# Linear attention and a Mish layer, gated: both halves of a block's query products in one group, E transposed in place, wo later

## The chip, the cores and the metric

The kernel runs on one core of a Trainium2 chip. The time is the device time of one execution in microseconds (us). Five engines work side by side, each through its own instructions in program order: PE (TensorE, the matmuls, which write to PSUM banks), DVE (VectorE), ACT (ScalarE), POOL (GpSimd) and SP (SyncE, which here only issues DMAs). They wait for each other by semaphores.

## What is computed

Inputs: x of 2048 rows and 512 columns, the weights of two branches, and a gate vector. Branch A is linear attention of 32 heads of 16 columns with a learned feature map, branch B two dense layers with Mish between them. All in float32.

```python
q, k, v = split(x @ wqkv)                       # 32 heads of 16
pq = einsum("bhsd,hdf->bhsf", q, w_phi); pk = einsum("bhsd,hdf->bhsf", k, w_phi)
phi_q = concat([softmax(pq), softmax(-pq)], -1) # 32 features a head
phi_k = concat([softmax(pk), softmax(-pk)], -1)
kv = einsum("bhsf,bhsd->bhfd", phi_k, v); z = einsum("bhsf->bhf", phi_k)
num = einsum("bhqf,bhfd->bhqd", phi_q, kv)
den = einsum("bhqf,bhf->bhq", phi_q, z)[..., None] + 1e-6
a = (num / den).reshape(B, S, D) @ wo
h = x @ w1 + b1                                 # 1376 hidden columns
b = (h * tanh(softplus(h))) @ w2
g = sigmoid((x * gate_w).sum(-1, keepdims=True))
out = g * a + (1 - g) * b
```

## The kernel before

The large products are made from split operands: each float32 matrix is written as h + l (a rounded high part and the rest), and a product is three: h·h, h·l, l·h. The small products with the features (`kv` and `nu`) take float32 as it is.

There are two stages. In stage A the 2048 rows go by in eight chunks of 256 rows (`a_ops`, two row tiles of 128 each): products `k`, `v`, `q` (`proj`, L232, twelve matmuls each), the features of k on DVE and ACT (`feat_ops`, L252), and `kv`, the sum over all rows of features times v (L322), which stays in one PSUM bank of its own (tag `kv`). The q products go to DRAM (`pqd`) and come back later. In stage B the rows go by in four blocks of 512 rows (`b_ops`, four row tiles t = 0 to 3): `up` (first dense layer, 11 pieces), Mish on ACT (`mi`, and `hi` for the high part), `lo` on POOL (L500), `dn` (second layer, four row tiles into four banks of tag `dn`), and for the attention branch the features of q. For a row tile t these are the steps

- `mx`, `mn`, `d0`, `d1` on DVE: row maxima and minima, and the differences for both softmaxes, written into a tile E (L265, L267); `E` on ACT: the exponent, in place
- `S`, `rS` (row sums and their reciprocals), `T`, `D`, `m`, `de`, `rd`, `sc` on DVE: the denominator (L553 to L579); `es` (L282): E scaled, in place; `tr` (L571): E transposed by blocks of 32 x 32 into a tile `tt`
- `mv` for a half h of the block (two row tiles): 16 DMAs on SP's queue, L591, which bring the pieces of `tt` into `eT`, with the features on partitions
- `nu` (L593): 16 products of `eT` with the kv matrix `kvb`, 64 rows by 32 columns of the array each, into two PSUM banks; `oh` on ACT and `ol` on DVE (L605, L610) copy them out as high and low part into two `ohl` tiles
- `wo` (L619, twelve matmuls) for one row tile, `ag` on ACT: scaled by the gate g into `io`; at the block's end `df` (last `dn`) and `fi` (the sum on DVE, and the DMA of the output on SP's queue)

`gr` brings the gate's logits of a block out of the first `up`, `ge` (ACT) and `gg` (DVE) make g and 1 - g. `LX`, `XH`, `XL` load the next block's x and split it (ACT, DVE); `XH` writes over the x of this block, so it stands behind the last `up`.

The order of all of it is written out by hand. Strings (`FIRST`, `EVEN`, `ODD`, `NEXT`, `LAST`, `BLOCK0`, `BLOCK1`, `BLOCK`) list the steps' names; `run` (L204) calls them in this order, and every instruction is pinned, so that each engine's own sequence follows it. A name with `+` belongs to the next block (chunk), with `'` to the one before. `BLOCK` serves blocks 2 and 3; in block 3 there is no next block, and the names with `+` do nothing. The tiles come from pools with a fixed number of buffers for each tag, and an instruction that writes a new tile waits for all readers of the tile that had the buffer. There are eight PSUM banks: four `dn`, three `a` (`k`, `q`, `up`, one bank of `nu`, `wo` of odd t) and one `kv` (the kv sum, then the other bank of `nu`, and `wo` of even t).

E had four buffers of one row tile (128 x 1024 float32), `tt` one and `eT` one of two row tiles (128 x 2048).

The features' tile, its transpose, the copies and the products:

```python
d["E"] = k4("E", "E")                                               # L262
pin(V.transpose(tts[h][:, t % 2, :, :].rearrange("p k x -> p (k x)"), d["E"][:, :]))   # L571
pin(Sy.dma_start(eTs[h][o : o + 32, :, q, :], tts[h][32 * q : 32 * q + 32, :, k, :]))  # L591
po = [psum("num", tag) for tag in ("kv", "a")]                       # L595
```

Of the kernel before, what the change touches and what calls it, by code (L numbers as in the profile page):

```python
# [15 lines left out]
P = 128  # L16
# [36 lines left out]
    S1 rS1 ml1 z1 v1 ve1 q0 mx0+ mn0+ d00+ d10+ qe0 st0 q1 qe1 st1 E0+ lq1+  # L53
"""
LAST = """
    k0 mx0 mn0 d00 d10 k1 E0 XH0 kv' mx1 mn1 d01 d11 E1 v0 S0 rS0 ml0 z0 ve0 ldo XH1 S1 rS1 ml1 z1 XL0 XL1
    v1 ve1 lq2+ mx1+ mn1+ d01+ d11+ q0 WH0 qe0 st0 q1 WH1 zh qe1 st1 E1+ zl kv S0+ rS0+ km
"""

# [3 lines left out]
    up0 mi0 hi0 lo0 gr lq3 S1 rS1 mx2 mn2 d02 d12 up1 @z mi1 hi1 lo1 T0 D0 m0 de0 rd0 sc0 es0 tr0 up2 mi2 hi2 lo2 dn0  # L63
    T1 D1 m1 de1 rd1 sc1 es1 tr1 mv0 lq0+ lq1+ mx3 mn3 d03 d13 up3 @kt mi3 hi3 lo3 dn1
    up4 mi4 hi4 lo4 WL0 dn2 E2 S2 T2 rS2 D2 m2 de2 rd2 sc2 es2 tr2 up5 mi5 hi5 lo5 WL1 dn3 E3 ge gg up6 mi6 hi6 lo6 dn4
    up7 mi7 hi7 lo7 dn5 nu0 oh0 S3 T3 rS3 ol0 D3 m3 de3 rd3 sc3 es3 tr3 mv1 up8 mi8 hi8 lo8 dn6
    mx0+ mn0+ d00+ d10+ mx1+ mn1+ d01+ d11+ lq2+ lq3+ wo0 ag0 wo1 ag1 E0+ E1+ S0+ T0+ rS0+ D0+ m0+ de0+ rd0+ sc0+ es0+ tr0+
    up9 mi9 hi9 lo9 dn7 up10 mi10 hi10 lo10 dn8 S1+ nu1 oh1 ol1 T1+ rS1+ D1+ LX0 LX1 m1+ de1+ rd1+ sc1+ es1+ tr1+ mv0+
    XH0+ XL0+ XH1+ XL1+ dn9 wo2 ag2 wo3 ag3 df0 fi0 df1 fi1 df2 fi2 df3 fi3
"""  # L70
BLOCK1 = """
    up0 mi0 hi0 lo0 gr mx2 mn2 d02 d12 mx3 mn3 d03 d13 up1 mi1 hi1 lo1 E2 E3 S2 T2 rS2 D2 m2 de2 rd2 sc2 es2 tr2
    up2 mi2 hi2 lo2 dn0 nu0 oh0 ol0 S3 T3 rS3 D3 m3 de3 rd3 sc3 es3 tr3 lq0+ lq1+ mv1 up3 mi3 hi3 lo3 dn1 up4 mi4 hi4 lo4 dn2
    mx0+ mn0+ d00+ d10+ mx1+ mn1+ d01+ d11+ lq2+ lq3+ up5 mi5 hi5 lo5 dn3 E0+ E1+ ge gg wo0 ag0 wo1 ag1
    S0+ T0+ rS0+ D0+ m0+ de0+ rd0+ sc0+ es0+ tr0+ up6 mi6 hi6 lo6 dn4 up7 mi7 hi7 lo7 dn5 nu1 oh1 ol1 S1+ T1+ rS1+ D1+ LX0 LX1
    m1+ de1+ rd1+ sc1+ es1+ tr1+ mv0+ mx2+ mn2+ d02+ d12+ mx3+ mn3+ d03+ d13+ up8 mi8 hi8 lo8 dn6 E2+ E3+
    wo2 ag2 wo3 ag3 up9 mi9 hi9 lo9 dn7 up10 mi10 hi10 lo10 dn8 XH0+ XL0+ XH1+ XL1+ dn9 df0 fi0 df1 fi1 df2 fi2 df3 fi3
"""
BLOCK = """
    up0 mi0 hi0 lo0 gr S2 T2 rS2 D2 m2 de2 rd2 sc2 es2 tr2 up1 mi1 hi1 lo1 up2 mi2 hi2 lo2 dn0 nu0 oh0 ol0  # L80
    S3 T3 rS3 D3 m3 de3 rd3 sc3 es3 tr3 lq0+ lq1+ mv1 up3 mi3 hi3 lo3 dn1 up4 mi4 hi4 lo4 dn2
    mx0+ mn0+ d00+ d10+ mx1+ mn1+ d01+ d11+ lq2+ lq3+ up5 mi5 hi5 lo5 dn3 E0+ E1+ ge gg wo0 ag0 wo1 ag1
    S0+ T0+ rS0+ D0+ m0+ de0+ rd0+ sc0+ es0+ tr0+ up6 mi6 hi6 lo6 dn4 nu1 oh1 ol1 S1+ T1+ rS1+ D1+ LX0 LX1 m1+ de1+ rd1+ sc1+
    es1+ tr1+ mv0+ up7 mi7 hi7 lo7 dn5 mx2+ mn2+ d02+ d12+ mx3+ mn3+ d03+ d13+ up8 mi8 hi8 lo8 dn6 E2+ E3+
    wo2 ag2 wo3 ag3 up9 mi9 hi9 lo9 dn7 up10 mi10 hi10 lo10 dn8 XH0+ XL0+ XH1+ XL1+ dn9 df0 fi0 df1 fi1 df2 fi2 df3 fi3
"""


# [1 line left out]
def tile_gated_mix(ctx: ExitStack, tc: tile.TileContext, xT, wv, wkT, wqT, bd, w1a, w1b, b1, w2a, w2b, wo, out):  # L90
# [14 lines left out]
        return sp.tile(shape, dt, name=f"{name}_{nm[0]}", tag=tag, bufs=bufs)  # L105

    def k8(name, tag, dt=F32R):
        return T([P, 2048], dt, tag, 1, name)

    def k4(name, tag, dt=F32):  # L110
        return T([P, 1024], dt, tag, {"E": 4, "tx": 2, "oh": 2, "z": 1}[tag], name)

    def k2(name, tag, dt=F32):
        return T([P, 512], dt, tag, {"pq": 3, "io": 4, "hl": 8}[tag], name)
# [8 lines left out]
    def kt(t, f):  # L123
        return t[:, : KT * f].rearrange("p (k f) -> p k f", f=f)
# [79 lines left out]
    def run(text, key, prev=None, nxt=None):  # L204
# [4 lines left out]


    wkh, wkl, wvh, wvl, wqh, wql = [
        kt(k8(n, t), 512) for n, t in (("wkh", "xbh"), ("wkl", "xbl"), ("wvh", "woh"), ("wvl", "wol"), ("wqh", "tt"), ("wql", "eT"))]
    xs, Es, vs, psA = {}, {}, {}, {}
    kvs = []
    zacc = k4("zacc", "z")
    pin(G_.memset(zacc, 0.0))
# [35 lines left out]
    def feat_ops(key, t, src, d):  # L252

        n = str(t)

        def red(name, op):
            d[name] = T([P, H], F32, name, 2, name)
            pin(V.tensor_reduce(d[name], hv(src()), axis=AX.X, op=op))  # L258

        def dd(a):  # L260
            if "E" not in d:
                d["E"] = k4("E", "E")  # L262
            E = hv(d["E"][:, a * 512 : (a + 1) * 512])
            if a == 0:
                pin(V.tensor_sub(E, hv(src()), d["mx"][:, :, None].to_broadcast([P, H, DH])))  # L265
            else:
                pin(V.tensor_sub(E, d["mn"][:, :, None].to_broadcast([P, H, DH]), hv(src())))  # L267

        def ss():
            d["S"] = T([P, 2 * H], F32, "Sm", 2, "Sm")  # L270
            pin(V.tensor_reduce(d["S"], hv(d["E"][:, :]), axis=AX.X, op=ALU.add))  # L271

        at(key, "mx" + n, lambda: red("mx", ALU.max))
        at(key, "mn" + n, lambda: red("mn", ALU.min))
        at(key, "d0" + n, lambda: dd(0))
        at(key, "d1" + n, lambda: dd(1))
        at(key, "E" + n, lambda: act(d["E"], d["E"], AF.Exp))
        at(key, "S" + n, ss)
        at(key, "rS" + n, lambda: pin(V.reciprocal(d["S"], d["S"])))
# [193 lines left out]

    def b_ops(b):
        key = ("B", b)
        U, dn, tts, eTs, num, ohl, io = {}, {}, {}, {}, {}, {}, {}

        def up(i):
            f = ORDER[i]
# [63 lines left out]
        for t in range(4):  # L543
            d = {}

            def lq(t=t, d=d):
                i = 4 * b + t
                d["p"] = k2("pq", "pq")
                pin(Sy.dma_start(d["p"], pqd[i * P : (i + 1) * P, :]))

            def tm(d=d):
                d["T"] = k4("T", "tx")
                pin(V.tensor_mul(d["T"], d["E"], B["zb"]))  # L553

            def dsum(d=d):
                d["D"] = T([P, 2 * H], F32, "Dn", 2, "Dn")
                pin(V.tensor_reduce(d["D"], hv(d["T"][:, :]), axis=AX.X, op=ALU.add))

            def de(d=d):
                d["d"] = T([P, H], F32, "den", 2, "den")  # L560
                pin(V.scalar_tensor_tensor(d["d"], d["D"][:, :H], 1e-6, d["D"][:, H:], op0=ALU.add, op1=ALU.add))

            def sc(d=d):
                sv = d["S"][:, :].rearrange("p (a h) -> p a h", a=2)
                pin(V.tensor_mul(sv, sv, d["d"][:, None, :].to_broadcast([P, 2, H])))

            def tr(t=t, d=d):
                h = t // 2
                if h not in tts:
                    tts[h] = k8("tt", "tt", F32)[:, :].rearrange("p (t k x) -> p t k x", t=2, k=4)  # L570
                pin(V.transpose(tts[h][:, t % 2, :, :].rearrange("p k x -> p (k x)"), d["E"][:, :]))  # L571

            at(key, f"lq{t}", lq)
            feat_ops(key, t, lambda d=d: d["p"][:, :], d)
            at(key, f"T{t}", tm)
            at(key, f"D{t}", dsum)
            at(key, f"m{t}", lambda d=d: pin(V.tensor_mul(d["D"], d["D"], d["S"])))
            at(key, f"de{t}", de)
            at(key, f"rd{t}", lambda d=d: pin(V.reciprocal(d["d"], d["d"])))  # L579
            at(key, f"sc{t}", sc)  # L580
            at(key, f"es{t}", lambda d=d: scale_by(d, V))
            at(key, f"tr{t}", tr)


        for h in range(2):
            def mv(h=h):
                eTs[h] = k8("eT", "eT", F32)[:, :].rearrange("p (t q x) -> p t q x", t=2, q=4)
                for q in range(4):
                    for k in range(4):
                        o = 64 * (k % 2) + 32 * (k // 2)  # L590
                        pin(Sy.dma_start(eTs[h][o : o + 32, :, q, :], tts[h][32 * q : 32 * q + 32, :, k, :]))  # L591

            def nu(h=h):  # L593
                ev = eTs[h][:, :, :, :].rearrange("p t q (b c) -> p b (t q) c", c=32)
                po = [psum("num", tag) for tag in ("kv", "a")]  # L595
                for bh in range(2):
                    for c in range(4):
                        u = 4 * bh + c
                        for r in range(2):
                            o = (u % 2) * 64 + 32 * r  # L600
                            mm(po[r][32 * c : 32 * c + 32, bh * SC : (bh + 1) * SC], kvb[64 * r : 64 * r + 64, u // 2, o : o + 32], ev[64 * r : 64 * r + 64, u, :, :], start=True, stop=True, skip_group_check=True)
                for r in range(2):
                    num[h, r] = po[r]

            def oh(h=h):  # L605
                for gp in range(2):
                    ohl[h, gp] = k4("ohl", "oh", F32R)
                    act(ohl[h, gp][:, :512], num[h, gp])

            def ol(h=h):  # L610
                for gp in range(2):
                    pin(V.tensor_sub(ohl[h, gp][:, 512:], num[h, gp], f32(ohl[h, gp][:, :512])))  # L612

            at(key, f"mv{h}", mv)
            at(key, f"nu{h}", nu)
            at(key, f"oh{h}", oh)
            at(key, f"ol{h}", ol)
# [192 lines left out]
```

## Time and profile before

| | |
|---|---|
| time, median of 3 runs | 451.06 us (450.77 to 451.5) |
| the profiled execution's own time | 451.0 us |
| its span, first to last instruction | 449.3 us |
| mean granted clock of TensorE | 0.999 |
| `num`, 128 products on PE (256 records) | 8.8 us |
| `wo` on PE | 10% of the chain |
| `up`, `dn` on PE | 27% and 26% of the chain |
| `tr` on DVE, 16 of them | 1.25 us each |
| `oh` on ACT, `ol` on DVE, 16 each | 0.59 us and 0.68 us each (median) |
| `lo` on POOL, 44 of them | 1.44 us each (mean) |

The span is what the profiler saw between the first and the last instruction of the core; the execution's time has 1.7 us more around it. A line of a timeline has the start in us from the span's start, the duration in us, the engine, the line of the code, the operation, the tile written and those read, the shapes, the count, and in brackets how long the engine had been idle before and what released it. PE lines have a duration that reaches past the start of the next matmul, since matmuls are pipelined: the step from one to the next is what one costs. Stage A ends, and block 0 begins, at about 151 us; blocks 1, 2 and 3 begin at 226.1, 299.4 and 372.6 us.

### The profile page before, as it was taken

The page shows a single profiled execution, that of the slowest core. Times are in us where ns is not written, and L with a number is a line of the kernel's source. Part 1 is how long each engine was busy: PE and PEld are TensorE (multiplying, and loading weights), DVE is VectorE, ACT ScalarE, POOL GpSimd, SP SyncE. Part 2 cuts the span into 40 slices and gives each one's busy share as a digit, 9 for nine tenths or more (in the row PEclk, how much of TensorE's full clock was granted, in tenths as well). Part 3 has the DMA queues.
Part 4 walks back from the last instruction along what each step waited for, and adds up shares of the span by engine and source line. Part 5 has one row for each costly group of instructions (what it writes and reads, how often), then busy time and mean ns, then how long its engine had stood idle before and what let it go on. Part 6 is the DMA issues. An engine that isn't in the chain of part 4 may idle for free.

```text
span 449.3 us, 7222 instructions
## 1 busy us (share of the span) xinstructions
PE 443.9 (99%) x2886; PEld 362.8 (81%) x2886; DVE 306.0 (68%) x408; ACT 195.0 (43%) x269; POOL 163.0 (36%) x102
## 2 busy tenths in 40 slices
PE   8999999999999999999999999999999999999997
PEld 7888888888888888878787887887887888787885
DVE  2798558459399999997979976476967529611003
ACT  3644533444325555627355453534253543244221
POOL 3448687677862345621122212014212122221211
PEclk9999999999999999999999999999999999999999
DMA  7721522514523111405143151331151302030002
GB/s 272 268 95 47 190 69 95 190 15 172 189 84 106 48 24 25 117 19 154 64 125 111 39 148 48 82 107 47 36 149 47 86 13 95 1 82 13 1 0 95
DMA packets 25883, 40.09 MB, mean 89 GB/s; under 512 B 5749, under 2 KB 14197, under 8 KB 25849
## 3 DMA queue, kind: packets, MB, share of 16 engines
q1 hardware_dynamic: 25528, 39.22, 28.6%
q8 instruction: 23, 0.38, 0.3%
q10 hardware_dynamic: 288, 0.39, 0.3%
q14 instruction: 12, 0.09, 0.1%
q0 software_dynamic: 32, 0.01, 0.0%
HBM read 22.82 MB, written 8.40 MB: 69 GB/s over the span
## 4 chain that ended last, share of the span: by engine, by line
PE 98%; DMA 1%; ACT 0%; DVE 0%; issue 0%
PE proj L101 29%; PE up L101 27%; PE down L101 26%; PE wo L101 10%; PE num L101 2%; PE kvp L101 2%; DMA bds<-in_bd_dram 1%; PE fuse L101 1%; PE rest L101 0%; PE z L101 0%; ACT wkh L121 0%; PE warm L101 0%; DVE io L653 0%; PE kvT L456 0%
## 5 line engine op out<-in xcount | busy, mean ns | idle before, releaser
L500 POOL TENSOR_TENSOR l<-act,h 128x512 fp32r<-128x512 f32 x44 | 63.2, 1438 | 221.9 <-ACT h L121 183.6
L121 ACT ACTIVATE act<-up,b1s 128x512 f32<-128x512 f32 x44 | 30.3, 688 | 89.0 <-PE up L101 88.8
L320 POOL TENSOR_TENSOR zacc<-zacc,E 128x1024 f32<-128x1024 f32 x16 | 39.7, 2483 | 42.7 <-DVE E L282 32.6
L121 ACT ACTIVATE E<-E 128x1024 f32<-128x1024 f32 x32 | 33.6, 1059 | 47.3 <-DVE E L267 44.3
L282 DVE TENSOR_TENSOR E<-E,Sm 128x1024 f32<-128x1024 f32 x32 | 45.7, 1427 | 1.1
L271 DVE TENSOR_REDUCE Sm<-E 128x64 f32<-128x1024 f32 x32 | 38.7, 1210 | 5.0 <-ACT E L121 5.0
L101 PE MATMUL wo<-woh,ohl 128*128 128x512 f32 x128 | 40.7, 389 | 0.0
L101 PE MATMUL down<-w2ah,h 128*128 128x512 f32 x96 | 37.5, 390 | 0.0
L101 PE MATMUL down<-w2al,h 128*128 128x512 f32 x96 | 37.4, 390 | 0.0
L101 PE MATMUL down<-w2ah,l 128*128 128x512 f32 x96 | 37.4, 389 | 0.0
L258 DVE TENSOR_REDUCE mx<-proj 128x32 f32<-128x512 f32 x16 | 11.0, 690 | 30.7 <-PE proj L101 30.7
L101 PE MATMUL down<-w2bh,h 128*128 128x512 f32 x78 | 30.5, 391 | 0.0
L101 PE MATMUL down<-w2bl,h 128*128 128x512 f32 x78 | 30.4, 390 | 0.0
L101 PE MATMUL down<-w2bh,l 128*128 128x512 f32 x78 | 30.4, 389 | 0.0
L121 ACT ACT_TABLE_LOAD x19 | 24.4, 1283 | 10.1 <-PE up L101 9.8
L121 ACT ACTIVATE h<-act 128x512 fp32r<-128x512 f32 x44 | 27.8, 632 | 1.4
L612 DVE TENSOR_TENSOR ohl<-num,ohl 128x512 fp32r<-128x512 f32 x16 | 10.3, 683 | 26.5 <-ACT ohl L121 26.3
L101 PEld LDWEIGHTS wo<-woh,ohl 128*128 128x128 f32 x128 | 24.0, 188 | 5.0
L101 PE MATMUL up<-xbh,w1ah 128*128 128x512 f32 x96 | 26.2, 395 | 0.0
L101 PE MATMUL up<-xbh,w1al 128*128 128x512 f32 x96 | 25.7, 390 | 0.0
L101 PE MATMUL up<-xbl,w1ah 128*128 128x512 f32 x96 | 25.7, 390 | 0.0
L405 DVE TENSOR_TENSOR xbl<-xraw,xbh 128x1024 fp32r<-128x1024 f32 x8 | 12.2, 1562 | 19.8 <-ACT xbh L121 19.8
(121 smaller groups left out, 966.6 us busy)
## 6 DMA issues: line engine op xcount, KB each, us to landing
eT<-tt SPq DMA_DIRECT2D x128, 64.0 KB, 2.0
xraw<-in_xT_dram SPq DMA_DIRECT2D x15, 512.0 KB, 4.4
pqd<-qs SPq DMA_DIRECT2D x16, 256.0 KB, 3.1
pq<-pqd SPq DMA_DIRECT2D x16, 256.0 KB, 2.9
out_dram<-io SPq DMA_DIRECT2D x15, 256.0 KB, 2.1
raw<-in_w1a_dram SPq DMA_DIRECT2D x3, 512.0 KB, 4.3
raw<-in_w2a_dram SPq DMA_DIRECT2D x3, 512.0 KB, 4.0
wT<-in_wkT_dram SPq DMA_DIRECT2D x4, 256.0 KB, 5.2
```

The source lines that it names most:

```text
L101: return pin(nc.tensor.matmul(*a, **k))
L121: return pin(A_.activation(out_, in_, fn, **k))
L258: pin(V.tensor_reduce(d[name], hv(src()), axis=AX.X, op=op))
L271: pin(V.tensor_reduce(d["S"], hv(d["E"][:, :]), axis=AX.X, op=ALU.add))
L282: pin(eng.tensor_mul(hv(d["E"][:, :]), hv(d["E"][:, :]), d["S"][:, :, None].to_broadcast([P, 2 * H, DH])))
L320: at(key, f"z{t}", lambda d=d: pin(G_.tensor_add(zacc, zacc, d["E"])))
L405: pin(V.tensor_sub(xb[b][1][:, :, sl], kt(raw[h], SC), f32(xb[b][0][:, :, sl])))
L500: pin(G_.tensor_sub(U[i]["l"], U[i]["a"], f32(U[i]["h"])))
L612: pin(V.tensor_sub(ohl[h, gp][:, 512:], num[h, gp], f32(ohl[h, gp][:, :512])))
```

## The change

Three things are done together. First, a row tile's E is half of a pair: one tile of 128 x 2048 for both row tiles of a chunk or of a half block, in two buffers in place of four single ones; `tr` transposes E onto itself, `mv` copies from the pair, and the room of `tt` goes to a second buffer of `eT`. Second, in each block `nu0` and `nu1` stand one behind the other: the first half has the banks `kv` and `a` as before, the second two banks of tag `a`, so that the group holds four banks (`kv` and all three `a`). Third, the order around it is written anew: `oh0` and `ol0` follow the group, `wo0` and `wo1` follow one `dn` later (in block 0 as well: `dn9`), then `oh1`, `ol1` and the next block's `tr1`, `mv0`, and `wo2` and `wo3` stand among the last `up` and `dn` (in block 0 behind `df`). In the last chunk of stage A `kv'` goes one `k` ahead.

```diff
 LAST = """
-    k0 mx0 mn0 d00 d10 k1 E0 XH0 kv' mx1 mn1 d01 d11 E1 v0 S0 rS0 ml0 z0 ve0 ldo XH1 S1 rS1 ml1 z1 XL0 XL1
+    k0 kv' mx0 mn0 d00 d10 k1 E0 XH0 mx1 mn1 d01 d11 E1 v0 S0 rS0 ml0 z0 ve0 ldo XH1 S1 rS1 ml1 z1 XL0 XL1
     v1 ve1 lq2+ mx1+ mn1+ d01+ d11+ q0 WH0 qe0 st0 q1 WH1 zh qe1 st1 E1+ zl kv S0+ rS0+ km
 """
...
-    up7 mi7 hi7 lo7 dn5 nu0 oh0 S3 T3 rS3 ol0 D3 m3 de3 rd3 sc3 es3 tr3 mv1 up8 mi8 hi8 lo8 dn6
-    mx0+ mn0+ d00+ d10+ mx1+ mn1+ d01+ d11+ lq2+ lq3+ wo0 ag0 wo1 ag1 E0+ E1+ S0+ T0+ rS0+ D0+ m0+ de0+ rd0+ sc0+ es0+ tr0+
-    up9 mi9 hi9 lo9 dn7 up10 mi10 hi10 lo10 dn8 S1+ nu1 oh1 ol1 T1+ rS1+ D1+ LX0 LX1 m1+ de1+ rd1+ sc1+ es1+ tr1+ mv0+
-    XH0+ XL0+ XH1+ XL1+ dn9 wo2 ag2 wo3 ag3 df0 fi0 df1 fi1 df2 fi2 df3 fi3
+    up7 mi7 hi7 lo7 dn5 S3 T3 rS3 D3 m3 de3 rd3 sc3 es3 tr3 mv1 up8 mi8 hi8 lo8 dn6
+    mx0+ mn0+ d00+ d10+ mx1+ mn1+ d01+ d11+ lq2+ lq3+ E0+ E1+ S0+ T0+ rS0+ D0+ m0+ de0+ rd0+ sc0+ es0+ tr0+
+    up9 mi9 hi9 lo9 dn7 up10 mi10 hi10 lo10 dn8 nu0 nu1 oh0 ol0 S1+ T1+ rS1+ D1+ LX0 LX1 m1+ de1+ rd1+ sc1+ es1+
+    dn9 wo0 ag0 XH0+ XL0+ wo1 ag1 oh1 ol1 tr1+ mv0+ df0 fi0 df1 fi1 df2 df3 XH1+ XL1+ wo2 ag2 wo3 ag3 fi2 fi3
 """
 BLOCK1 = """
     up0 mi0 hi0 lo0 gr mx2 mn2 d02 d12 mx3 mn3 d03 d13 up1 mi1 hi1 lo1 E2 E3 S2 T2 rS2 D2 m2 de2 rd2 sc2 es2 tr2
-    up2 mi2 hi2 lo2 dn0 nu0 oh0 ol0 S3 T3 rS3 D3 m3 de3 rd3 sc3 es3 tr3 lq0+ lq1+ mv1 up3 mi3 hi3 lo3 dn1 up4 mi4 hi4 lo4 dn2
-    mx0+ mn0+ d00+ d10+ mx1+ mn1+ d01+ d11+ lq2+ lq3+ up5 mi5 hi5 lo5 dn3 E0+ E1+ ge gg wo0 ag0 wo1 ag1
-    S0+ T0+ rS0+ D0+ m0+ de0+ rd0+ sc0+ es0+ tr0+ up6 mi6 hi6 lo6 dn4 up7 mi7 hi7 lo7 dn5 nu1 oh1 ol1 S1+ T1+ rS1+ D1+ LX0 LX1
-    m1+ de1+ rd1+ sc1+ es1+ tr1+ mv0+ mx2+ mn2+ d02+ d12+ mx3+ mn3+ d03+ d13+ up8 mi8 hi8 lo8 dn6 E2+ E3+
-    wo2 ag2 wo3 ag3 up9 mi9 hi9 lo9 dn7 up10 mi10 hi10 lo10 dn8 XH0+ XL0+ XH1+ XL1+ dn9 df0 fi0 df1 fi1 df2 fi2 df3 fi3
+    up2 mi2 hi2 lo2 dn0 S3 T3 rS3 D3 m3 de3 rd3 sc3 es3 tr3 lq0+ lq1+ mv1 up3 mi3 hi3 lo3 dn1 up4 mi4 hi4 lo4 dn2
+    mx0+ mn0+ d00+ d10+ mx1+ mn1+ d01+ d11+ lq2+ lq3+ up5 mi5 hi5 lo5 dn3 E0+ E1+ ge gg
+    S0+ T0+ rS0+ D0+ m0+ de0+ rd0+ sc0+ es0+ tr0+ up6 mi6 hi6 lo6 dn4 up7 mi7 hi7 lo7 dn5 nu0 nu1 oh0 ol0 S1+ T1+ rS1+ D1+ LX0 LX1
+    m1+ de1+ rd1+ sc1+ es1+ dn6 wo0 ag0 wo1 ag1 oh1 ol1 tr1+ mv0+ dn7 up8 mi8 hi8 lo8 mx2+ mn2+ d02+ d12+ mx3+ mn3+ d03+ d13+
+    wo2 ag2 up9 mi9 hi9 lo9 dn8 E2+ E3+ up10 mi10 hi10 lo10 wo3 ag3 XH0+ XL0+ XH1+ XL1+ dn9 df0 fi0 df1 fi1 df2 fi2 df3 fi3
 """
 BLOCK = """
-    up0 mi0 hi0 lo0 gr S2 T2 rS2 D2 m2 de2 rd2 sc2 es2 tr2 up1 mi1 hi1 lo1 up2 mi2 hi2 lo2 dn0 nu0 oh0 ol0
+    up0 mi0 hi0 lo0 gr S2 T2 rS2 D2 m2 de2 rd2 sc2 es2 tr2 up1 mi1 hi1 lo1 up2 mi2 hi2 lo2 dn0
     S3 T3 rS3 D3 m3 de3 rd3 sc3 es3 tr3 lq0+ lq1+ mv1 up3 mi3 hi3 lo3 dn1 up4 mi4 hi4 lo4 dn2
-    mx0+ mn0+ d00+ d10+ mx1+ mn1+ d01+ d11+ lq2+ lq3+ up5 mi5 hi5 lo5 dn3 E0+ E1+ ge gg wo0 ag0 wo1 ag1
-    S0+ T0+ rS0+ D0+ m0+ de0+ rd0+ sc0+ es0+ tr0+ up6 mi6 hi6 lo6 dn4 nu1 oh1 ol1 S1+ T1+ rS1+ D1+ LX0 LX1 m1+ de1+ rd1+ sc1+
-    es1+ tr1+ mv0+ up7 mi7 hi7 lo7 dn5 mx2+ mn2+ d02+ d12+ mx3+ mn3+ d03+ d13+ up8 mi8 hi8 lo8 dn6 E2+ E3+
-    wo2 ag2 wo3 ag3 up9 mi9 hi9 lo9 dn7 up10 mi10 hi10 lo10 dn8 XH0+ XL0+ XH1+ XL1+ dn9 df0 fi0 df1 fi1 df2 fi2 df3 fi3
+    mx0+ mn0+ d00+ d10+ mx1+ mn1+ d01+ d11+ lq2+ lq3+ up5 mi5 hi5 lo5 dn3 E0+ E1+ ge gg
+    S0+ T0+ rS0+ D0+ m0+ de0+ rd0+ sc0+ es0+ tr0+ up6 mi6 hi6 lo6 dn4 nu0 nu1 oh0 ol0 S1+ T1+ rS1+ D1+ LX0 LX1 m1+ de1+ rd1+ sc1+
+    es1+ dn5 wo0 ag0 wo1 ag1 oh1 ol1 tr1+ mv0+ dn6 up7 mi7 hi7 lo7 wo2 ag2 mx2+ mn2+ d02+ d12+ mx3+ mn3+ d03+ d13+
+    up8 mi8 hi8 lo8 dn7 E2+ E3+ up9 mi9 hi9 lo9 wo3 ag3 up10 mi10 hi10 lo10 dn8 XH0+ XL0+ XH1+ XL1+ dn9 df0 fi0 df1 fi1 df2 fi2 df3 fi3
 """
...
     def k8(name, tag, dt=F32R):
-        return T([P, 2048], dt, tag, 1, name)
+        return T([P, 2048], dt, tag, 2 if tag in ("eT", "E") else 1, name)
...
             if "E" not in d:
-                d["E"] = k4("E", "E")
+                pair = key, t // 2
+                if pair not in Ep:
+                    Ep[pair] = k8("E", "E", F32)[:, :].rearrange("p (t x) -> p t x", t=2)
+                d["E"] = Ep[pair][:, t % 2, :]
...
-            def tr(t=t, d=d):
-                h = t // 2
-                if h not in tts:
-                    tts[h] = k8("tt", "tt", F32)[:, :].rearrange("p (t k x) -> p t k x", t=2, k=4)
-                pin(V.transpose(tts[h][:, t % 2, :, :].rearrange("p k x -> p (k x)"), d["E"][:, :]))
+            def tr(d=d):
+                pin(V.transpose(d["E"][:, :], d["E"][:, :]))
...
-                        pin(Sy.dma_start(eTs[h][o : o + 32, :, q, :], tts[h][32 * q : 32 * q + 32, :, k, :]))
+                        pin(Sy.dma_start(eTs[h][o : o + 32, :, q, :], Ep[key, h][32 * q : 32 * q + 32, :, k * 256 : (k + 1) * 256]))
...
-                po = [psum("num", tag) for tag in ("kv", "a")]
+                po = [psum("num", tag) for tag in (("kv", "a"), ("a", "a"))[h]]
```

More of the change, by code (lines that the diff above doesn't have):

```diff
@@ L107, in k8 @@
     def k8(name, tag, dt=F32R):
-        return T([P, 2048], dt, tag, 1, name)
+        return T([P, 2048], dt, tag, 2 if tag in ("eT", "E") else 1, name)
     def k4(name, tag, dt=F32):
-        return T([P, 1024], dt, tag, {"E": 4, "tx": 2, "oh": 2, "z": 1}[tag], name)
+        return T([P, 1024], dt, tag, {"tx": 2, "oh": 2, "z": 1}[tag], name)
     def k2(name, tag, dt=F32):
@@ L211, in tile_gated_mix @@
     wkh, wkl, wvh, wvl, wqh, wql = [
-        kt(k8(n, t), 512) for n, t in (("wkh", "xbh"), ("wkl", "xbl"), ("wvh", "woh"), ("wvl", "wol"), ("wqh", "tt"), ("wql", "eT"))]
-    xs, Es, vs, psA = {}, {}, {}, {}
+        kt(k8(n, t), 512) for n, t in (("wkh", "xbh"), ("wkl", "xbl"), ("wvh", "woh"), ("wvl", "wol"), ("wqh", "eT"), ("wql", "eT"))]
+    xs, Es, vs, psA, Ep = {}, {}, {}, {}, {}
     kvs = []
@@ L475, in b_ops @@
         key = ("B", b)
-        U, dn, tts, eTs, num, ohl, io = {}, {}, {}, {}, {}, {}, {}
+        U, dn, eTs, num, ohl, io = {}, {}, {}, {}, {}, {}
         def up(i):
```

## The prediction

> **What bounds the kernel now.** I read first the page's parts 1, 2 and 4 (busy shares, slices, the chain that ended last), then the waits of PE, then the timelines of PE, DVE, ACT, POOL and SP from 100 us on.
>
> ```profile
> PE 443.9 (99%) x2886; PEld 362.8 (81%) x2886; DVE 306.0 (68%) x408; ACT 195.0 (43%) x269; POOL 163.0 (36%) x102
> PEclk9999999999999999999999999999999999999999
> PE 98%; DMA 1%; ACT 0%; DVE 0%; issue 0%
> ```
>
> PE (TensorE) is the chain: 98% of it, at full clock, and the view of waits gives PE 2.1 us of waiting in all, all of it before 40 us. So the change can gain only by making PE's own work shorter, and loses whatever wait it brings to PE. Nothing that DVE, ACT or POOL saves counts by itself.
>
> A block of PE's work is made of equal pieces: twelve matmuls of 512 columns, one each 0.2267 us (213.55 to 213.78 below), so an `up`, one `dn` (four tiles of three products) or a `wo` takes 2.72 us.
>
> **Part 1: eight small groups become four double ones.** A group of products with `kvb` (`nu`) beside full ones, from PE's timeline:
>
> ```profile
> 213.78 0.39 PE L101 MATMUL down<-w2bh,l 128*128 128x512 f32 x1
> 214.10 1.09 PE L101 MATMUL num<-eT,kvb 64*32 64x256 f32 x32
> 215.12 0.50 PE L101 MATMUL down<-w2bh,h 128*128 128x512 f32 x1
> 215.46 0.40 PE L101 MATMUL down<-w2bl,h 128*128 128x512 f32 x1
> ...
> 113.32 1.07 PE L101 MATMUL proj<-wqh,xl 128*128 128x512 f32 x4
> 114.32 1.99 PE L101 MATMUL kvp<-E,v 128*32 128x64 f32 x128
> 116.24 1.20 PE L101 MATMUL proj<-wkh,xh 128*128 128x512 f32 x4
> 117.28 1.07 PE L101 MATMUL proj<-wkl,xh 128*128 128x512 f32 x4
> ```
>
> Without the group, the second `down` after it would start 0.45 us after 213.78, at 214.23; it starts at 215.46: the group costs 1.23 to 1.24 us. The double group is not in the blocks, but the A stage has one of the same length per instruction: `kv'` and `kv` of two chunks back to back (x128). Four products from 113.32 end at 114.23; the next four should end 0.91 later, and the second four start at 117.28, so the double group costs 117.28 - 114.23 - 0.91 = 2.14 us, while the single `kv` at 138.22 costs 1.24. Two singles less one double is 2 x 1.24 - 2.14 = 0.33 us. Four blocks: **-1.3 us**. That is the whole of the gain; the bounds are 0 (the two halves do not join) and -1.4.
>
> **Part 2: E transposed in place, pairs of E.** The transpose (1.25 us, x16) keeps its size and its shape; `tt` is gone and `eT` has two buffers. DVE, SP and their counts stay: 16 transposes, 128 copies of 64 KB into `eT`. An in-place read and write is in no row; 0 and +1.25 us each on DVE (as if it ran twice) are the bounds, and I take 0, since the exponent and the scaling of E (L121, L282) also work in place at the time of their size. A pair of E is now freed as a whole and after its copies. For A chunks the `kv` that frees it is done before the next chunk's first `k`; in blocks the copies of a half end tens of us before the next pair needs the place. That is why `kv'` of the last chunk must go ahead: it moves by one `k` (2.72 us), its price of 1.24 is the same. Behind it DVE waits for `k1`, which ends 1.24 later (DVE's idle time at 138.33 was for PE), and the x of block 0 (`XL1`) then ends at 151.92 + 1.24 = 153.16, against its first reader on PE at 153.33: hidden, with 0.1 us to spare. DVE starts block 0 late by 1.24; by its third row tile I have it late by 0.2 only, because several of its products had waited for POOL (T at 168.83 lasts 2.12 instead of 1.21 us) and wait less when they come later.
>
> **Part 3: the second half of `nu` in block 0.** There `nu1` now stands right behind `nu0`, ahead of `dn9` and `wo0`, `wo1`, and so earlier. What it reads comes through DVE's transpose of tile 3 and 16 copies on SP's queue (timelines of DVE and SP; the last line is of the page's part 6, its last number the us to landing):
>
> ```profile
> 192.98 1.29 DVE L612 TENSOR_TENSOR ohl<-num,ohl 128x512 fp32r<-128x512 f32 x2
> 194.19 1.21 DVE L557 TENSOR_REDUCE Dn<-T 128x64 f32<-128x1024 f32 x1
> ...
> 196.56 1.23 DVE L282 TENSOR_TENSOR E<-E,Sm 128x1024 f32<-128x1024 f32 x1
> 197.82 1.25 DVE L571 STREAM_TRANSPOSE tt<-E 128x1024 f32<-128x1024 f32 x1
> 199.14 10.18 SPq L591 DMA_DIRECT2D eT<-tt  x16
> eT<-tt SPq DMA_DIRECT2D x128, 64.0 KB, 2.0
> ```
>
> Before, the last copy is issued near 199.14 + 15 x 0.636 = 208.7 and lands 2.0 later, at 210.7; `nu1` at 214.10 had 3.4 us to spare. After: PE loses from ahead of the group `nu0` (1.24) and `wo0`, `wo1` (5.44), so the group starts at 214.10 - 6.68 = 207.42 and its second half wants to at 207.42 + 0.91 = 208.33. DVE loses `ol0` (1.21, the two rows' step at 192.98) ahead of tile 3: its D at 193.0, its scaling (L282) at 195.39, the transpose ends at 197.9, the last copy lands at 209.5. PE waits **1.2 us**. The scaling is close to a race: POOL's `lo8`, after an `up8` that is 1.24 earlier, wants to start at 195.47. Such rows exclude each other, as this pair shows:
>
> ```profile
> 253.60 1.29 POOL L500 TENSOR_TENSOR l<-act,h 128x512 fp32r<-128x512 f32 x1 [4.14 <-ACT h L121]
> ...
> 254.03 1.41 DVE L265 TENSOR_TENSOR E<-pq,mx 128x512 f32<-128x512 f32 x1
> ```
>
> The DVE row lasts 1.41 us instead of 0.68, and its last 0.55 us lie behind POOL's end at 254.89. If `lo8` is first, the scaling waits to 196.76, the copies land at 210.9 and PE waits 2.6 us. I take 1.6, nearer to the end where DVE keeps its lead of 0.08 us; the bounds are 0 (the DVE chain a further 1.2 us early) and 2.6. Then `ol0` is not late there: `wo0` comes at 212.19 + 1.6, and `ol0` by 212 to 213.3.
>
> The Trainium skill ("SBUF — State Buffer", section "Who interferes with whom") says that a VectorE instruction with two SBUF inputs and a GpSimd one that reads SBUF hold a shared pair of ports one at a time, each for the whole of its instruction, the first to start going first. The pair of rows above agrees (254.03 to 255.44 around 254.89). By that rule the wait is either 1.2 or 2.6 us and nothing between them.
>
> **Part 4: `wo0` behind `ol0` in block 2.** All four banks of `nu` must be copied (ACT, `oh`) and subtracted (DVE, `ol`) before PE can go on in them, and `wo0` writes the bank that `ol0` reads first. In block 2 only `dn5` stands between the group and `wo0`, and `ol0` stands on DVE behind the whole of the next block's tile 0 (S to the transpose), which begins with E's exponent and the gate:
>
> ```profile
> 325.33 0.69 ACT L121 ACTIVATE act<-up,b1s 128x512 f32<-128x512 f32 x1 [4.09 <-PE up L101]
> ...
> 329.91 0.19 ACT L121 ACTIVATE ge_sb<-ge_sb 128x4 f32<-128x4 f32 x1
> 330.63 1.21 DVE L271 TENSOR_REDUCE Sm<-E 128x64 f32<-128x1024 f32 x1
> 336.94 1.25 DVE L571 STREAM_TRANSPOSE tt<-E 128x1024 f32<-128x1024 f32 x1
> 340.58 1.29 DVE L612 TENSOR_TENSOR ohl<-num,ohl 128x512 fp32r<-128x512 f32 x2 [2.40 <-ACT ohl L121]
> ```
>
> Count from the end of `up5` (325.07 here). S starts 330.63 - 325.07 = 5.56 later, for ACT's table load, two exponents and `ge` lie between; this stays. From S to the end of the transpose 7.48 to 7.56, and 0.2 for POOL's `lo6`, which is now beside it. So the first row of `ol0` (0.68) ends at 5.56 + 7.7 + 0.68 = 13.95. PE: `dn3`, `up6`, `dn4`, the group, `dn5` are 4 x 2.72 + 2.14 = 13.02. With 0.1 us for the signal (as from 138.11 to ACT's 138.21) PE waits **1.0 us**; bounds 0.6 (the row of `lo6` misses it, the signal costs nothing, the group costs 0.2 more) and 1.3. Before, `ol0` had the time of `up3` and `dn1`, and `nu1` came after the transpose anyway. Block 1 has `up7` and `dn6` more between them: there the same sum leaves 0.3 to 1.8 us free, and nothing waits. Block 3 has no next block on DVE: free by 1.6. The second `oh`, `ol` of each block have `wo1`'s and a `dn`'s time; the tightest (block 2, `up7` into the third bank) has 0.4 us.
>
> The remaining moves (`wo2`, `wo3`, `XH`, `XL` in block 0 ahead of `oh1`, `ag`) put the same rows elsewhere: the second x half of block 1 ends near 226 against a reader after 227.6; `mi9` in block 0 is late by 3 us for the exponents ahead of it on ACT, but its product is read at 209.5. I cost them at 0; if that cover went, each would cost up to 1.3.
>
> **The sum.** -1.3 + 1.6 (block 0) + 1.0 (block 2) = +1.3 us. The profiled execution took 451.0 us (its span is 449.3, so 1.7 lie around it); the median of the runs is 451.06, the same within 0.1. Forecast: **452.3 us**, 0.3% slower. About 0.2%, 0.9 us, is what a measurement here can tell from no change.
>
> **Rivals.**
> A. The copies land in time and `ol0` is done in time: the gain alone, 451.0 - 1.3 = 449.7. It decides if tile 3's transpose in block 0 ends before 196.6 and `ol0` in block 2 ends 1 us earlier than I count. For it: DVE's shift in block 0 rests on races with POOL that I cannot settle; against: block 2's chain is paced by ACT and its parts have steady rows. 15%.
> B. Only one of the two waits is there: 451.0 - 1.3 + (1.0 to 1.6) = 450.7 to 451.3, no change. For it: block 0's copies have 1.2 us to win from five waits between DVE and POOL. 25%.
> C. POOL wins the race in block 0, and block 1's `ol0`, with 0.3 us free at worst, is late too by the same kind of row (up to 0.9): 451.0 - 1.3 + 2.6 + 1.0 + (0 to 0.9) = 453.3 to 454.2. 12%.
> D. The groups do not join: the second half waits for its banks or copies, PE empties between them, and nothing is saved in some block. That is worth 0.33 us a block and lies inside the other cases.
>
> The forecast itself (452.0 to 453.0): 48%. Slower 0.60, same 0.25, faster 0.15. The range 450.3 to 453.8 holds the forecast, B and most of C; A lies outside. The forecast's own range is 452.0 to 453.0.
>
> **What would show it.** In the changed profile: four groups of `num` with x64 and some 2.1 us of PE each, instead of eight of 1.1; PE waiting for `eT`'s copies once, inside the group of block 0, for 1.2 or 2.6 us; PE waiting for DVE's `ohl` at the first `wo` of block 2, about 1 us, and in no other block. I am wrong if PE's waits after 150 us sum to less than 1.3 us, or if a wait stands at another place (an `up` behind the third bank, `dn0` behind the outputs).

## The result, and the profile after

The changed kernel takes 452.67 us (median of 11 runs, 451.97 to 454.62), the kernel before 450.96 us beside it (450.61 to 451.5): a ratio of 1.0038, with a 95% interval of 1.003 to 1.0045. It is slower by 1.7 us.

The profiled execution took 452.72 us with a span of 450.9, 1.6 more than the span before. The lines that answer to the first ones of before, from the page's parts 1, 2 and 4:

```profile
PE 444.1 (98%) x2886; PEld 363.9 (81%) x2886; DVE 308.8 (68%) x408; ACT 195.0 (43%) x269; POOL 163.7 (36%) x102
PE 73%; DVE 18%; SPq 3%; DMA 2%; issue 1%; ACT 1%
```

PE's work is the same, at full clock (mean granted clock 1.000). But the chain that ended last is no longer PE alone: DVE holds 18% of it and SP's queue 3%. In a chain followed back from the end this does not mean that DVE set 18% of the time; it means that at two places PE was let go by another engine, and the chain then runs back along that one for a while. The view of PE's waits names the two places:

```profile
PE num L101 <- DMA eT<-E: 1.4, 1, 1.4
PE warm L101 <- DVE ones L170: 1.1, 1, 1.1
PE wo L101 <- DVE ohl L612: 0.7, 1, 0.7
PE proj L101 <- ACT wkh L121: 0.3, 1, 0.3
```

The second and fourth line were there before, in the first 40 us. The first and the third are new. Their sizes are too small, because a matmul's modelled end reaches past the start of the next; the steps between starts are a better measure. Taken from PE's timeline, from the first `up` of a block to the first `up` of the next (block 3: to the first `rest`):

| | before | after | difference |
|---|---|---|---|
| stage A, to the first `up` | 151.39 | 151.19 | -0.20 |
| block 0 | 74.74 | 76.64 | +1.90 |
| block 1 | 73.21 | 72.87 | -0.34 |
| block 2 | 73.21 | 73.85 | +0.64 |
| block 3 | 71.85 | 71.51 | -0.34 |

The sum is +1.66 us. Stage A's 0.20 is there from the first `fuse` on (6.02 before, 5.81 after), which waits for the first loads, and is no effect of the change. Blocks 1 and 3 have the gain of the joined groups and nothing else. So block 0 waits 1.90 + 0.34 = 2.24 us, block 2 waits 0.64 + 0.34 = 0.98 us.

Block 0's place in PE's timeline, then SP's and DVE's (start, duration, engine, operation, tiles):

```profile
207.24 1.09 PE L101 MATMUL num<-eT,kvb 64*32 64x256 f32 x32
209.69 1.75 PE L101 MATMUL num<-eT,kvb 64*32 64x256 f32 x32 [1.36 <-DMA eT<-E]
211.37 0.50 PE L101 MATMUL down<-w2bh,h 128*128 128x512 f32 x1
...
194.94 1.23 DVE L285 TENSOR_TENSOR E<-E,Sm 128x1024 f32<-128x1024 f32 x1
196.20 1.25 DVE L571 STREAM_TRANSPOSE E<-E 128x1024 f32<-128x1024 f32 x1
195.29 2.03 POOL L503 TENSOR_TENSOR l<-act,h 128x512 fp32r<-128x512 f32 x1 [4.14 <-ACT h L121]
197.50 11.34 SPq L591 DMA_DIRECT2D eT<-E  x16
205.17 1.76 SPq L591 DMA_DIRECT2D eT<-E  x1
```

The second half of the group wants to start at 207.24 + 0.91 = 208.15. It starts at 209.69, and is itself longer (1.75 instead of 1.09): its first two records come at 209.69 and 209.90, and the third at 210.35, 0.09 us after the last copy lands (210.26). The scaling of E (L285) is ahead of POOL's `lo` by 0.35 us; POOL waits for it (2.03 instead of 1.3 us). The 16 copies are issued from 197.50 on, but in 11.34 us instead of 10.18: one issue, at 205.17, takes 1.76 us instead of 0.59.

Block 2's place, PE and DVE:

```profile
333.44 1.96 PE L101 MATMUL num<-eT,kvb 64*32 64x256 f32 x64
...
337.99 0.39 PE L101 MATMUL down<-w2ah,l 128*128 128x512 f32 x1
339.06 0.50 PE L101 MATMUL wo<-woh,ohl 128*128 128x512 f32 x1 [0.68 <-DVE ohl L612]
...
330.73 1.22 DVE L274 TENSOR_REDUCE Sm<-E 128x64 f32<-128x1024 f32 x1
337.18 1.25 DVE L571 STREAM_TRANSPOSE E<-E 128x1024 f32<-128x1024 f32 x1
338.35 1.25 DVE L612 TENSOR_TENSOR ohl<-num,ohl 128x512 fp32r<-128x512 f32 x2
```

The double group is one of x64. `wo0` would follow at 338.22; `ol0` starts at 338.35, right behind the transpose of the next block's tile 0, its first row (0.65 to 0.69 us) ends near 339.0, and PE goes on at 339.06.

### The profile page after: what moved, and what is told of

Read it like the earlier page. It is cut to its first block, busy times and chain, and to the rows that moved or that the text cites. A ratio compares the mean times of both kernels' runs of the same rounds, so it can differ in the third digit from the quotient of the medians.

```text
span 450.9 us, 7217 instructions
## 1 busy us (share of the span) xinstructions
PE 444.1 (98%) x2886; PEld 363.9 (81%) x2886; DVE 308.8 (68%) x408; ACT 195.0 (43%) x269; POOL 163.7 (36%) x102
## 4 chain that ended last, share of the span: by engine, by line
PE 73%; DVE 18%; SPq 3%; DMA 2%; issue 1%; ACT 1%
PE proj L101 27%; PE down L101 16%; PE up L101 16%; PE wo L101 10%; SPq L591 3%; DVE T L556 2%; DVE E L285 2%; DVE Sm L274 2%; DVE E L571 2%; DVE Dn L560 2%; PE kvp L101 2%; DVE xbl L408 1%; PE num L101 1%; DMA bds<-in_bd_dram 1%; DVE Sm L282 1%
## 5 line engine op out<-in xcount | busy, mean ns | idle before, releaser
L285 DVE TENSOR_TENSOR E<-E,Sm 128x1024 f32<-128x1024 f32 x32 | 46.6, 1456 | 1.1
L121 ACT ACTIVATE io<-wo,g_sb 128x512 f32<-128x512 f32 x16 | 11.0, 690 | 43.8 <-PE wo L101 43.8
```

Of the source, the lines that this page charges most:

```text
L121: return pin(A_.activation(out_, in_, fn, **k))
L285: pin(eng.tensor_mul(hv(d["E"][:, :]), hv(d["E"][:, :]), d["S"][:, :, None].to_broadcast([P, 2 * H, DH])))
```

## The experiments

Each is compared with the kernel before on the same chip.

**`ol0` first, in block 2.**

```diff
-    S0+ T0+ rS0+ D0+ m0+ de0+ rd0+ sc0+ es0+ tr0+ up6 mi6 hi6 lo6 dn4 nu0 nu1 oh0 ol0 S1+ T1+ ...
+    S0+ T0+ rS0+ D0+ m0+ de0+ rd0+ sc0+ up6 mi6 hi6 lo6 dn4 nu0 nu1 oh0 ol0 es0+ tr0+ S1+ T1+ ...
```

> The changed kernel, with one edit in the order of blocks 2 and 3: on DVE, ol0 stands ahead of the next block's es0 and tr0 instead of behind them. Theory (PE waits in block 2 because ol0 stands behind the whole of the next block's tile 0 on DVE): ol0's first row then ends near 336.6 on the changed kernel's time line, ahead of the 338.1 at which PE wants wo0; block 2 shortens from 73.85 us to 72.9 (its 73.21 before, less 0.33), blocks 0, 1 and 3 stay, and the time falls by 1.0 from 452.7 to 451.7. Rival (the 0.7 to 1.0 us at wo0 is a bank or a product that is late for another reason, such as POOL's lo): block 2 stays at 73.85 and the time at 452.7.

Measured: 451.47 us, ratio 1.0012 (1.0003 to 1.0021), 1.2 us less than the changed kernel in its own runs. Block 2 takes 72.87 us; blocks 1 and 3 are as they were, block 0 takes 76.45. DVE and PE in this run:

```profile
335.98 1.28 DVE L612 TENSOR_TENSOR ohl<-num,ohl 128x512 fp32r<-128x512 f32 x2
337.18 1.22 DVE L285 TENSOR_TENSOR E<-E,Sm 128x1024 f32<-128x1024 f32 x1
...
338.16 0.39 PE L101 MATMUL down<-w2ah,l 128*128 128x512 f32 x1
338.39 0.39 PE L101 MATMUL wo<-woh,ohl 128*128 128x512 f32 x1
```

`ol0` now starts before the scaling, and `wo` follows `dn` by 0.23 us, the step of any matmul. The wait was `ol0`'s place on DVE.

**The group one `dn` later, in block 0.**

```diff
-    ... dn8 nu0 nu1 oh0 ol0 S1+ ... es1+
-    dn9 wo0 ag0 XH0+ XL0+ wo1 ag1 oh1 ol1 tr1+ mv0+ df0 fi0 df1 fi1 df2 df3 XH1+ XL1+ wo2 ...
+    ... dn8 dn9 nu0 nu1 oh0 ol0 S1+ ... es1+
+    df0 df1 wo0 ag0 XH0+ XL0+ wo1 oh1 ag1 ol1 tr1+ mv0+ fi0 fi1 df2 df3 XH1+ XL1+ wo2 ...
```

> The changed kernel, with block 0's order changed alone: the group of eight banks' products stands one dn later (behind dn9), half of the last dn (df0, df1) covers ol0, the other half (df2, df3) covers ol1, and oh1 goes ahead of ag1. Theory (PE waits in block 0 for the 16 copies into eT behind tile 3's transpose): the copies land near 210.3, the second half of the group now wants them near 210.9, nothing waits; block 0 falls from 76.64 to 74.4 us (74.74 before, less 0.33) and the time by 2.2 to 450.5. Rival (block 0 is longer because of the order of ACT and DVE there, the exponents ahead of mi9 and mi10 or wo's place): block 0 stays above 76 and the time near 452.7.

Measured: 451.24 us, ratio 1.0006 (0.9997 to 1.0015). Block 0 falls to 75.06 us, by 1.6 and not by 2.2. The wait for the copies is gone (the group is one of x64 at 210.44), but a new one of 0.5 us has come: see below.

**Both.**

> Both of these edits in the changed kernel. Theory: only the gain of the joined groups is left, 0.33 us in each of four blocks: 451.0 - 1.3 = 449.7 us, below the kernel before by 0.3%, with PE waiting nowhere after 150 us. Rival (joining saves nothing, the double group costs as much as two single ones): 451.0, the same as before.

Measured: 450.26 us, ratio 0.9985 (0.9976 to 0.9994): block 0 75.06, blocks 1 and 2 72.87 each, block 3 71.51. In the blocks' lengths the two edits add up, and what is left of the change is a small gain: the interval ends below 1. The expectation's "waiting nowhere" was missed, at one place of block 0:

```profile
220.47 0.39 PE L101 MATMUL wo<-wol,ohl 128*128 128x512 f32 x1
221.18 0.73 PE L101 MATMUL wo<-woh,ohl 128*128 128x512 f32 x2 [0.32 <-DVE ohl L612]
...
219.31 1.22 DVE L408 TENSOR_TENSOR xbl<-xraw,xbh 128x1024 fp32r<-128x1024 f32 x1
220.44 1.28 DVE L612 TENSOR_TENSOR ohl<-num,ohl 128x512 fp32r<-128x512 f32 x2
```

The third product of `wo2` needs the low part of `ohl`. `ol1` had its banks and its high parts by 219.7, but it stands behind `XL0` on DVE.

**Only the tiles: pairs of E, in place, `kv'` earlier; blocks in the order of before.** The strings `BLOCK0`, `BLOCK1` and `BLOCK` and the banks of `nu` are those of before, the rest is the changed kernel's.

> The order of the blocks and the banks of nu as before, with the pairs of E, the transpose in place, the two buffers of eT and kv' one k earlier kept. Theory (these cost nothing): 451.0 us, within 0.2% of before, 16 transposes of 1.25 us. Rival (part of the 1.7 us is theirs: the transpose in place is slower, or a pair is freed late): 451.5 to 452.7.

Measured: 451.07 us, ratio 1.0003 (0.9994 to 1.0011). Blocks take 74.77, 73.21, 73.21 and 71.85 us, as before within 0.03. The transpose, before and here, in the view of groups (busy us, mean ns):

```profile
L571 DVE STREAM_TRANSPOSE tt<-E 128x1024 f32<-128x1024 f32 x16 | 19.9, 1246 | 0.6
```

```profile
L571 DVE STREAM_TRANSPOSE E<-E 128x1024 f32<-128x1024 f32 x16 | 19.9, 1246 | 0.6
```

The mean is the same. All of the 1.7 us comes from the order of the blocks and the banks that go with it.

**Both, and `XL0` behind `ol1`.**

```diff
-    df0 df1 wo0 ag0 XH0+ XL0+ wo1 oh1 ag1 ol1 tr1+ mv0+ ...
+    df0 df1 wo0 ag0 XH0+ wo1 oh1 ag1 ol1 XL0+ tr1+ mv0+ ...
```

> The version with both edits (late group in block 0, ol0 first in block 2), and one more in block 0: XL0 of the next block stands behind ol1 on DVE, not ahead of it. Theory (the 0.65 us that block 0 has over 74.4 is wo2 waiting for ol1, which stands behind XL0's 1.2 us): block 0 falls from 75.06 to 74.4 to 74.5 us, no wait of PE is left after 150 us, and the time from 450.26 to 449.7. Rival (the late order has another cost): block 0 stays at 75.06, the time at 450.3.

Measured: 449.67 us, ratio 0.997 (0.9959 to 0.9981): faster than the kernel before by 1.25 us in its own runs. Blocks take 74.44, 72.87, 72.87 and 71.51 us, each 0.30 to 0.34 less than before. PE's waits, all of them:

```profile
PE warm L101 <- DVE ones L170: 1.1, 1, 1.1
PE fuse L101 <- DMA bds<-in_bd_dram: 0.8, 1, 0.8
PE proj L101 <- ACT wkh L121: 0.3, 1, 0.3
```

Nothing is left after the first 40 us. This version is faster than the kernel before by 0.3%.

**The long issue.** In the changed kernel a packet of 16 KB of the queue that the page lists as "q8 instruction" starts at 205.16 us and lasts 1.3 us, in the middle of the copies, and the long issue starts with it. This run moves the packets against the copies.

```diff
-WARM = 10
+WARM = 38
...
-            mm(pw[:, :P], ones, ones, start=True, stop=True)
+            mm(pw[:, :32], ones, ones[:, :32], start=True, stop=True)
```

> The changed kernel with 38 small warm-up matmuls (32 columns) at the start in place of 10 (128 columns), so that PE's instruction stream is some 7 KB longer from there on; nothing else differs. In the changed kernel's trace a 16 KB packet of the instruction queue q8 at 205.2 falls into the 16 copies of block 0, and one of their issues lasts 1.76 us instead of 0.59. Theory (q8 carries PE's instructions, and such a packet holds up SP's issue of a copy): the packet comes some 10 us earlier, outside of the copies, they take 10.2 us instead of 11.3, and block 0 falls from 76.64 to about 75.5 us. Rival (the long issue comes from what else runs at that point, or by chance): the copies of block 0 still take 11.1 to 11.4 us and block 0 76.4 to 76.7. The time itself may differ by up to 1 us at the start and isn't the measure here; block 0's length is.

Measured: no packet falls into block 0's copies, block 0 takes 75.47 us, and blocks 1, 2 and 3 take the changed kernel's 72.87, 73.85 and 71.51. SP's queue there, and PE:

```profile
211.34 10.18 SPq L591 DMA_DIRECT2D eT<-E  x16
...
221.07 1.09 PE L101 MATMUL num<-eT,kvb 64*32 64x256 f32 x32
222.37 1.75 PE L101 MATMUL num<-eT,kvb 64*32 64x256 f32 x32 [0.20 <-issue]
```

The copies take 10.18 us again. Their row starts 9.73 us ahead of the group here and 9.74 us in the changed kernel, so up to the copies the two blocks are alike. On PE the second half of the group starts 1.30 us after the first (221.07 to 222.37) where the changed kernel needed 2.45 (207.24 to 209.69). In all block 0 is 1.07 us late: 75.47 less the 74.40 of a block 0 without waits (74.74 - 0.34). With the packet the long issue has gone, then, and with it 1.17 us of block 0 (76.64 less 75.47); the other 1.07 us come from the order. The run with `ol0` first, whose block 0 is the changed kernel's, has the packet among these copies too, with an issue of 1.54 us and a block 0 of 76.45. Where it fell in the executions that were not profiled is not on record. The time itself was missed by far: 465.32 us (one run) instead of at most 1 more, for the warm-up; see the last section.

## Why the prediction was right

The forecast was 452.3 us, and each of its terms stayed within its bounds. One term, block 0's copies, came out larger than taken, and about half of it for a reason that the forecast did not have.

- **The joined groups, -0.33 a block:** measured -0.34 in blocks 1 and 3, and in all four blocks (-0.30 to -0.34) where no wait covers it. The forecast took stage A's double group as the model for it, and the step it gave held.
- **E in place, pairs, `kv'`: 0.** Measured +0.1 us with an interval across zero. `XL1` ends at 148.40 + 4.55 = 152.95 against its reader at 153.14: 0.2 us to spare, about what was worked out (153.16 against 153.33). The lag of DVE, 0.2 us by its third row tile, was gone at the next one, t = 3: its S starts at 189.71 after and 189.89 before, the difference being that of the whole stage.
- **Block 0's copies, 1.2 or 2.6, taken as 1.6:** measured 2.24. The mechanism and the place were right, and the later group removes the wait. The race of E's scaling with POOL went to DVE, as in the case of 1.2 us, and by more than the 0.08 us given (194.94 against 195.29), mostly because DVE's lag had gone. Where the forecast let the two exclude each other, by its pair of rows and by the Trainium skill ("SBUF — State Buffer", section "Who interferes with whom": the first to start holds the ports for its whole instruction), this trace agrees: POOL's row ends at 197.32, 1.15 us after the scaling ends at 196.17. But the consequence drawn from it, 1.2 or 2.6 us and nothing between, did not hold. The step that failed is the price of the copies behind it: the forecast put 0.636 us on each issue, and one took 1.76. Without that, 1.07 us are left, near the 1.2 of the sum. So the term, taken as 1.6, was too small by 0.64 us, and what it allowed for above 1.2 was the lost race, which did not happen, and not the long issue, which did. That the time still fell between 452.0 and 453.0 is luck in part: without the long issue it would have been near 451.5 (an estimate, 452.67 - 1.17), below the forecast's own range.
- **`wo0` behind `ol0` in block 2, 1.0:** measured 0.98, and gone when `ol0` goes first.
- **The rest at 0:** no other wait in the changed kernel; the first row of block 1's `ol0` ended 1.3 us ahead of its `wo0`, at the upper side of the 0.3 to 1.8 given. But the cover that was named (the time of `wo1` and a `dn`) shows its limit once block 0 is moved: `ol1` behind `XL0` then costs 0.6 us.
- **The rivals:** both waits are there, so A and B fall. C falls with POOL's lost race and with block 1's `ol0`, which was in time. D, worth 0.33 us a block, can be seen in block 0 alone: there the halves stand as two rows of x32 with PE idle between them. Whether the 0.34 us was saved there can't be told apart from the wait; the 2.24 us counts it as saved, and without it the wait is 1.90.

The sum with measured terms: -0.20 (start) - 4 x 0.34 + 2.24 + 0.98 = 1.66, as in the table; the spans differ by 1.6.

## What to carry to other kernels

Joining two groups of small products that use the array in parts saved 0.33 us a block here (two groups of 1.24 us against a double one of 2.14 in the forecast's model), but brings both halves' inputs and both halves' outputs to one point: read off when the last input lands and which engine's queue the first copy-out stands in. Where PE has no wait at all, the order on the other engines is what a reordering of PE is paid with; a copy-out that frees a bank goes ahead of work for the next block. Behind a row of 16 DMA issues a margin under some 1.3 us was not safe in these runs: the row took 10.2 us without a long issue and up to 11.5 with one, which lasted two to three times as long as the others.

## What the runs showed of the hardware that was not expected

- **A long DMA issue comes with an instruction packet.** Over the eight profiled kernels there are 64 rows of 16 copies on SP's queue. A 16 KB packet of q8 starts inside 17 of them, and each of these 17 has one issue of 1.1 to 1.9 us (0.59 otherwise), which starts within 0.3 us of the packet, and takes 10.7 to 11.5 us; of the other 47 none has an issue above 0.74 us, and they take 10.2 to 10.6. More instructions on PE ahead of block 0 moved the packet out of block 0's copies (in one run), and block 0's row went back to 10.18 us. That q8 carries PE's instructions fits this, but it is inferred from it; why an issue waits for such a packet no run here shows.
- **The narrow warm-up matmuls were no cheaper, and PE came to its later pace later.** A float32 warm-up matmul is two records. At the start of the kernel a record of 128 columns takes 0.213 us from start to start in the changed kernel (20 of them), and one of 32 columns takes 0.213 us in the run with 38 matmuls (76 of them, 16.42 us in all). The 28 more matmuls are thus 12.0 of the 12.7 us by which the span is longer. That the width doesn't matter is not shown by this: the weights loaded for each record are 128 x 128 in both runs, and both ran at a slow pace. In the changed kernel a warm-up record of 128 columns at 6.64 us takes 0.112 us, while in the other run products of 512 columns still take 0.427 us each at 21.2 to 22.5 us and 0.23 us from 22.8 us on. Why the pace changes that much later there is open.
